# A third PSUM pair and an order by due times in a backward decode step of attention and gated MLP

## The chip, the cores and the metric

The kernel runs on one core of a Trainium2 chip. The metric is the device time of one execution in microseconds (us). Five engines work in parallel, each through its own queue in the order in which instructions were written: TensorE (PE, matmuls and weight loads), ScalarE (ACT), VectorE (DVE), GpSimd (POOL) and SyncE (SP, which here only issues DMAs). An instruction whose input or buffer isn't ready holds up everything behind it on its engine.

## The reference

For one decode token of two batches, output and all gradients of `x + attention(LN(x)) + MLP(LN(x))` are computed. The parts that carry the time:

```python
B, Sq, D, Hq, Hkv, Sk, Dh, F = 2, 1, 576, 32, 16, 4096, 128, 4608
scores = einsum("bhqd,bhkd->bhqk", q, k) * Dh**-0.5      # q = (xn @ wq), k, v: caches, each KV head for 2 query heads
o = einsum("bhqk,bhkd->bhqd", softmax(scores), v)        # attention = o @ wo
h = (xn @ w_gate) * (xn @ w_up)                          # MLP = h @ w_down
_out, _vjp = jax.vjp(f, x, k_cache, v_cache, wq, wo, w_gate, w_up, w_down)
return (_out, *_vjp(grad_out))
```

The caches are 2 x 16 x 4096 x 128 in bf16, 1 MB for each head and batch and cache. Their gradients are as large and are outer products: dV = p times dO, dK = dS times q. The gradients of the weights are outer products too.

## The kernel before, in words

**Steps.** The work on the caches is cut into 16 steps (`NS`): 8 groups of two KV heads (`G`), for each of the two batches. A step loads four tiles of 1 MB (`load_kv`, K and V of two heads, ring `kv` of 9 buffers), turns them on VectorE with 32-bit transposes (`turn`, ring `X` of 3), makes the scores of K (`score` with t=0, into PSUM tile `sk`) and the softmax (`softmax`), then the same product of V with dO (`dscore`, tile `sv`) and dS. `spread` brings p and dS into the forms `pp` and `dd` with small matmuls. `contract` then multiplies `pp` with V and `dd` with K, 128 matmuls, for the step's part of o and dq; only after it are the step's four `kv` buffers free for new loads. `outer` and `head_outer` make dV from `pp` and dK from `dd`: for each of 2 heads and 2 gradients four units (`unit`), 16 in a step. A unit takes a pair of PSUM banks (ring `o`, 2 pairs), fills it with two matmuls of 512 columns, and ScalarE or VectorE copies ("evicts") its 1024 columns to a store tile `st` (ring of 4). After four units the 1 MB tile is stored by SP. The right operand `BD` of the units is built by GpSimd, two for each step (L909).

**Weights.** Each group of heads also has a `group_front` (q and dO from the weights) and a `group_back` (gradients of wq and wo); nine `mlp` blocks of 512 columns of F do the MLP. Their outer products use the same `unit`s: `rows_unit` (576 columns), `cols_unit` (1024) and the tails (256).

**Small PSUM tiles.** The tiles `sk` and `sv` have a bank each; everything else that is small takes turns in ring `m` of two banks.

**What sets the order.** All functions are generators. `Order.run` simulates five engines with a fixed cost for each operation and writes the instructions in the order in which its simulated engines take them. Where several generators could go on at about the same time (`SLACK` 0.15), the lower priority number wins: scores and loads 0.0, stores 0.5, `contract` 1.0, `turn` 1.0, `mlp` 1.5, every outer unit 2.0. `EV` picks the engine of an eviction by the simulated time. Loads and stores of the caches share SP's queue (L810 and L477); loads of weights are on it as well; stores of weight gradients are on GpSimd's queue.

Of the kernel before, what the change touches and what calls it, by code (L numbers as in the profile page):

```python
# [13 lines left out]
P = 128  # L14
# [20 lines left out]
class Order:  # L35
# [3 lines left out]
    SLACK = 0.15  # L39

    def __init__(self):
        self.free = {e: 0.0 for e in ("PE", "ACT", "DVE", "POOL", "SP")}
        self.busy = dict(self.free)
        self.slots = {}
        self.dma = 0.0
        self.streams = []
        self.count = 0
        self.log = []
# [10 lines left out]
    def advance(self, s, value):  # L59
        while True:  # L60
# [13 lines left out]
            elif kind == "now":  # L74
                value = s.ready
# [31 lines left out]
    def run(self):  # L107
        while self.streams:
            cand = []
            for s in self.streams:  # L110
                t, e = self.start(s)
                if t is not None:
                    cand.append((t, s, e))
            assert cand, "no stream can go on: %s %s" % (
                [(x.gen.__name__, x.gen.gi_frame.f_lineno, x.ready, x.req) for x in self.streams], self.slots)
            t0 = min(c[0] for c in cand)
            t, s, e = min((c for c in cand if c[0] <= t0 + self.SLACK), key=lambda c: (c[1].prio, c[0]))
            r = s.req
            value = None
            if r[0] in ("op", "any"):  # L120
                cost = r[2] if r[0] == "op" else next(c for x, c, _ in r[1] if x == e)
                self.free[e] = t + cost
                self.busy[e] += cost
                s.ready = t + cost + self.HOP
                self.log.append((t, cost, e, s.prio))
# [9 lines left out]
            elif r[0] == "dma":  # L135
                self.free[e] = t + r[2]
                self.busy[e] += r[2]
# [3 lines left out]
                self.log.append((t, r[2], e, s.prio))  # L141
# [23 lines left out]
def EV(cols, bias=0.25):  # L165
    return ("any", [("ACT", 0.19 + cols * 0.00083, 0.0), ("DVE", 0.16 + cols * 0.00104, bias)])
# [21 lines left out]

def DMA(engine, cost, nbytes):
# [5 lines left out]
MLP0, MLPD = 5, 6.5  # L195
KVSTORE = "SP"


@with_exitstack
def kernel(  # L200
# [79 lines left out]
    osb_t = tiles("osb", 1, [P, P], FP32)  # L280
    od.ring("ch", 2)
    ch_t = []
    for i in range(2):
# [5 lines left out]
            pr=const.tile([P, P], BF16, name=f"pr{i}"), cs=const.tile([P, 1], FP32, name=f"cs{i}"),  # L289
            cr=const.tile([P, 1], FP32, name=f"cr{i}"), ds=const.tile([P, P], BF16, name=f"ds{i}")))  # L290
# [52 lines left out]
    for be in range(4):  # L343
        nc.vector.tensor_copy(sel[:, be], view(ident[:], 0, P, 64 * (be // 2) + be % 2, [[0, 4], [2, 32]]))
        nc.vector.tensor_copy(selA[:, be], view(ident[:], 0, P, 32 * be, [[0, 4], [1, 32]]))
    one1 = const.tile([1, 1], FP32, name="one1")
    nc.vector.memset(one1[:], 1.0)
    zer = const.tile([1, P], BF16, name="zer")
    nc.vector.memset(zer[:], 0.0)
# [12 lines left out]
    Wdy = const.tile([P, NB, 2, P], BF16, name="Wdy")  # L362
# [17 lines left out]
    def front():  # L380
# [37 lines left out]
        for src, dst in ((yb, dyr), (xnb, xnr)):  # L418
# [9 lines left out]
            if dst is dyr:  # L428
# [4 lines left out]
                for a in range(4):  # L433
                    nc.vector.tensor_copy(
                        view(Wdy[:], 32 * a, 32, 32 * a, [[P, 2 * NB], [1, 2]]), dyT[32 * a:32 * a + 32, :, 0:2])
# [28 lines left out]
    class Store:  # L464
        def __init__(self, n, out, after=None):
            self.n, self.out, self.after = n, out, after

        def done(self):
            self.n -= 1
            if self.n == 0:  # L470
                yield SPAWN(self.out(), (0.5,))
# [11 lines left out]
    def unit(mms, pe, cols, ev, store):  # L483
        i = yield ACQ("o")
        yield PE(pe)
# [19 lines left out]
    def rows_unit(a, lhs, st):  # L505
        def mms(o):
            for k in range(2):
                nc.tensor.matmul(o[:, k, 0:HD2], lhsT=lhs(a), rhs=dyr[32 * a:32 * a + 32, k * HD2:(k + 1) * HD2],  # L508
                                 start=True, stop=True)

        def ev(e, o):
            cp(e, st[:, a * D:(a + 1) * D].rearrange("p (k n) -> p k n", k=2), o[:, :, 0:HD2])
        return mms, 0.45, D, ev

    def rows_outer(lhs, dst, events=()):
# [3 lines left out]
        store = Store(FC, put("POOL", [(dst, src, 128 * FC * D * 2)], "st", i, events))  # L519
        for a in range(FC):  # L520
            yield SPAWN(unit(*rows_unit(a, lhs, st), store), (2.0,))

    def cols_outer(rhs, dst, events=()):
# [3 lines left out]
        store = Store(2, put("POOL", [(dst, src, 128 * 4 * FS * 2)], "st", i, events))  # L527
        for A in range(2):
            yield SPAWN(unit(*cols_unit(A, rhs, st, 0), store), (2.0,))

    def tail_outer(rhss, dsts, events=()):
# [4 lines left out]
        store = Store(2, put("POOL", parts, "tl", i, events))  # L536
# [12 lines left out]
        for A in range(2):  # L549
            yield SPAWN(unit(*mk(A), store), (2.0,))  # L550
# [6 lines left out]
    def mlp(i, Lgu, Ld, gs_slot, wd_slot):  # L557
# [26 lines left out]
        for k in range(NB):  # L584
            for e in range(2):
                nc.tensor.matmul(
                    dh, lhsT=Wdy[:, k, e, :], rhs=view(X[:], 0, P, 64 * k + e, [[D, FC], [2, 32]]),
# [10 lines left out]

        E = [Event() for _ in range(4)]
        yield SPAWN(rows_outer(lambda a: hb[32 * a:32 * a + 32, 0, :],  # L600
                               out_8[f0:f0 + FS, :].rearrange("(a p) n -> p a n", p=P), (E[0],)), (2.0,))
        for w, out in enumerate((out_6, out_7)):
            yield SPAWN(cols_outer(lambda a, w=w: hb[32 * a:32 * a + 32, 1 + w, :],
                                   out[0:512, f0:f0 + FS].rearrange("(c p) n -> p c n", p=P), (E[1 + w],)), (2.0,))
        yield SPAWN(tail_outer([lambda a, w=w: hb[32 * a:32 * a + 32, 1 + w, :] for w in range(2)],
                               [out[512:576, f0:f0 + FS] for out in (out_6, out_7)], (E[3],)), (2.0,))
# [18 lines left out]
        yield PE(1.6)  # L625
# [37 lines left out]
    def group_front(g):  # L663
# [7 lines left out]
        yield PE(1.6)  # L671
# [34 lines left out]
        for k in range(NB):  # L706
            for e in range(2):
                nc.tensor.matmul(
                    dp, lhsT=Wdy[:, k, e, :], rhs=view(X[:], 0, P, 64 * k + e, [[D, GH], [2, 32]]),
# [14 lines left out]
    def group_back(g):  # L724
# [9 lines left out]
        for t in range(2):  # L734
            for h in range(GH):
# [4 lines left out]
        E = [Event() for _ in range(3)]  # L740
        yield SPAWN(rows_outer(lambda a: R[32 * a:32 * a + 32, 0, :],
                               out_5[n0:n0 + FS, :].rearrange("(h p) n -> p h n", p=P), (E[0],)), (2.0,))
# [476 lines left out]
```

## Time and profile before

| | |
|---|---|
| median of 3 runs | 639.78 us (638.91 to 640.46) |
| profiled execution | 640.2 us, its span 638.4 us |
| mean granted TensorE clock | 0.584 of full |
| moved by DMA | 186.20 MB, mean 292 GB/s |
| evictions of 1024 columns | ScalarE 284, VectorE 24 |
| first and last `contract` matmul start | 42.7 and 578.3 us |

The span runs from the first to the last instruction. "Busy" is the time in which an engine had an instruction running; a group's line names the kernel's line, the engine, the operation, out<-in, and a count, then its busy time and the mean of one in ns, then the idle time of the engine just before and what ended it. In a timeline, the bracket gives the idle time before a row and its releaser; for SP a row can span the waits between the DMAs that it merges. "DMA share" is the mean busy share of the core's 16 DMA engines.

### The profile page before, as it was taken

What the parts mean: (1) busy time and instruction counts of PE and PEld (TensorE: products, weight loads), DVE (VectorE), ACT (ScalarE), POOL (GpSimd) and SP (SyncE); (2) the same over time, 40 slices, a digit from 0 to 9 for tenths busy, and PEclk for the clock granted to TensorE, in tenths of its full rate; (3) what the DMA queues carried; (4) which work ended last, traced back from release to release, by engine and by line L of the source; (5) the groups of instructions that cost most, each with busy time, mean ns of one, the idle gap of its engine ahead of it and who ended that gap; (6) DMA issues with size and microseconds to landing.
All of it is one profiled execution on the core that took longest, in us unless ns stands there. A gap on an engine that the chain in (4) does not pass through costs nothing. (4 is left out here: it accounts for less than half of the span.)

```text
span 638.4 us, 19297 instructions
## 1 busy us (share of the span) xinstructions
PE 452.2 (71%) x8489; PEld 270.5 (42%) x8489; DVE 355.1 (56%) x643; ACT 344.5 (54%) x470; POOL 204.8 (32%) x289
## 2 busy tenths in 40 slices
PE   1597676868767784778787775847687587978662
PEld 1475452635325452555354341424455454435210
DVE  8889631794227934688176552417395398344005
ACT  0124447564774664556544847656552176675890
POOL 4462033433314422343232323321154035332200
PEclk9976565765557565755555565655557555556555
DMA  8949989693998749986963969896938965493661
GB/s 314 377 165 360 381 322 411 234 382 144 364 390 353 295 179 397 373 334 191 393 282 137 402 269 397 315 377 254 333 135 328 378 229 208 181 343 150 243 268 78
DMA packets 47532, 186.20 MB, mean 292 GB/s; under 512 B 4396, under 2 KB 23992, under 8 KB 31064
## 3 DMA queue, kind: packets, MB, share of 16 engines
q1 hardware_dynamic: 40424, 159.61, 65.4%
q0 software_dynamic: 7024, 25.37, 10.4%
q8 instruction: 66, 1.08, 0.7%
q14 instruction: 18, 0.15, 0.1%
HBM read 92.48 MB, written 92.48 MB: 290 GB/s over the span
## 5 line engine op out<-in xcount | busy, mean ns | idle before, releaser
L309 ACT CAST st<-ps_o 128x1024 bf16<-128x1024 f32 (+1 forms) x345 | 310.6, 958 | 155.9 <-PE ps_o L953 74.8
L909 POOL TENSOR_TENSOR BD<-vr,mask 128x2048 bf16<-128x2048 bf16 x32 | 115.1, 3598 | 150.0 <-PE ps_o L953 102.5
L305 DVE STREAM_TRANSPOSE X<-kv 128x1024 f32<-128x1024 f32 x128 | 152.1, 1218 | 10.3 <-DMA kv<-in_A_k_cache_dram 6.0
L953 PE MATMUL ps_o<-BD,dd 32*128 32x512 bf16 x256 | 71.8, 592 | 31.1 <-ACT st L309 29.9
L953 PE MATMUL ps_o<-BD,pp 32*128 32x512 bf16 x256 | 68.5, 551 | 26.2 <-ACT st L309 25.5
L311 DVE CAST st<-ps_o 128x1024 bf16<-128x1024 f32 (+1 forms) x31 | 34.5, 1114 | 70.9 <-PE ps_o L508 29.3
L477 POOL DMA_DIRECT2D out_dram<-st x43 | 33.2, 771 | 94.1 <-ACT st L309 87.7
L921 PEld LDWEIGHTS <-W 128*32 128x32 bf16 x2048 | 50.4, 132 | 25.7 <-issue 22.7
L1092 PE MATMUL ps_m<-kv,dd 128*2 128x128 bf16 x1024 | 53.7, 286 | 5.0 <-issue 5.0
L1092 PE MATMUL ps_m<-kv,pp 128*2 128x128 bf16 x1024 | 53.6, 286 | 3.0 <-issue 3.0
L305 DVE STREAM_TRANSPOSE X<-ww 128x1152 f32<-128x1152 f32 x25 | 34.2, 1369 | 32.5 <-DMA ww<-in_B_w_down_dram 30.4
L1092 PEld LDWEIGHTS <-pp 128*2 128x2 bf16 x1024 | 45.0, 111 | 8.5 <-issue 7.0
L1092 PEld LDWEIGHTS <-dd 128*2 128x2 bf16 x1024 | 45.0, 111 | 5.9 <-issue 5.9
L953 PEld LDWEIGHTS <-dd 32*128 32x128 bf16 x256 | 15.0, 103 | 63.3 <-issue 57.5
L953 PEld LDWEIGHTS <-pp 32*128 32x128 bf16 x256 | 14.7, 99 | 58.8 <-issue 55.3
L888 POOL COPY W<-rep 32x16 bf16<-32x16 bf16 x128 | 24.5, 192 | 46.8 <-DVE rep L692 40.4
L921 PE MATMUL ps_sk<-X,W 128*32 128x128 bf16 x1024 | 31.7, 297 | 9.8 <-DVE X L305 9.2
L921 PE MATMUL ps_sv<-X,W 128*32 128x128 bf16 x1024 | 30.8, 296 | 4.0 <-DVE X L305 2.7
L448 POOL COPY wt<-wm 64x128 bf16<-64x128 bf16 (+1 forms) x34 | 8.9, 263 | 58.6 <-DVE wm L442 52.1
L477 POOL DMA_DIRECT2D out_dram<-tl x26 | 14.6, 563 | 33.0 <-ACT tl L309 33.0
L508 PE MATMUL ps_o<-dyr,R 32*128 32x288 bf16 x64 | 18.1, 394 | 9.0 <-ACT st L309 8.7
L309 ACT CAST vr<-ps_m 128x128 bf16<-128x128 f32 x19 | 5.1, 268 | 35.2 <-PE ps_m L901 35.2
(178 smaller groups left out, 593.3 us busy)
## 6 DMA issues: line engine op xcount, KB each, us to landing
out_dram<-st SPq DMA_DIRECT2D x64, 1024.0 KB, 6.1
kv<-in_A_k_cache_dram SPq DMA_DIRECT2D x32, 1024.0 KB, 11.3
kv<-in_A_v_cache_dram SPq DMA_DIRECT2D x32, 1024.0 KB, 9.5
out_dram<-st POOLq DMA_DIRECT2D x26, 512.0 KB, 7.7
out_dram<-st POOLq DMA_DIRECT2D x17, 576.0 KB, 8.1
ww<-in_B_w_down_dram SPq DMA_DIRECT2D x9, 576.0 KB, 8.3
ww<-in_A_wo_dram SPq DMA_DIRECT2D x8, 576.0 KB, 7.9
gu<-in_B_w_gate_dram SPq DMA_DIRECT2D x9, 512.0 KB, 10.0
```

Source lines behind the costliest of these rows:

```text
L305: nc.vector.transpose(out, in_)
L309: nc.scalar.copy(out, in_)
L311: nc.vector.tensor_copy(out=out, in_=in_)
L448: nc.gpsimd.tensor_copy(view(Wt[:], 64 * h, 64, 0, [[dims[-1][1], n], [1, dims[-1][1]]]), view(Wm[:], 64 * h, 64, off, dims))
L477: (nc.gpsimd if engine == "POOL" else nc.sync).dma_start(dst, src)
L508: nc.tensor.matmul(o[:, k, 0:HD2], lhsT=lhs(a), rhs=dyr[32 * a:32 * a + 32, k * HD2:(k + 1) * HD2], start=True, stop=True)
L888: nc.gpsimd.tensor_copy(view(W_t[t][w][:], 32 * a, 32, 6 + 8 * a, [[G * WW, 4], [WW, G], [1, 2]]), view(rep_t[grp[g]["qs"]][:], 32 * a, 32 ...
L909: nc.gpsimd.tensor_tensor(BD_t[i][:], view(vr_t[v][:], 0, P, 0, [[0, 16], [1, Dh]]), view(mask16[:], 0, P, 0, [[1, 16], [0, Dh]]), ALU.mult)
L921: nc.tensor.matmul(sc[32 * cq:32 * cq + 32, :], lhsT=view(W[:], 0, P, (be * G + l) * WW + 6 - 4 * c2 - 2 * l, [[1, 32]]), rhs=view(X[:], 0 ...
L953: nc.tensor.matmul(o[:, k, :], lhsT=pr2[32 * c4:32 * c4 + 32, :], rhs=BD[32 * c4:32 * c4 + 32, 8 * l + 4 * h2:8 * l + 4 * h2 + 4, :], star ...
L1092: nc.tensor.matmul(ct[32 * j:32 * j + 2, 0:P], lhsT=rT[:, 4 * c + 2 * l:4 * c + 2 * l + 2], rhs=kv_t[slot][:, Dh * c:Dh * (c + 1)], start= ...
```

## The change

**Third pair.** The tiles `sk` and `sv` are gone, and ring `o` has three pairs. The scores now lie in ring `m`. So that a score tile is read from PSUM once, the maximum is taken by an operation that also copies the tile to `ex` in SBUF, and the exponential works there in place. In `dscore` the tile is read once into `ed` (`ex` times dP), and dS comes from two VectorE operations on SBUF tiles.

**Quadrants.** A unit of dK or dV uses row quadrants 0 and 1 or 2 and 3 of TensorE. Units now alternate between the two halves, and the planner counts the second of such a pair at 0.12. `rows_unit` takes two quadrants where it took one twice.

**Fewer small products.** `contract` uses 32 columns of the weights for each head and no longer a zero matmul ahead. The transpose after it is in bf16, its two copies are one. `Wdy` is stored overlapped.

**Order.** Each stage of each step has a due time, `STEP * s + PR[name]`, as its priority; the two queues of weight loads are apart; `SLACK` is a number for each engine, and the planner takes the earliest start first. `turn` and the evictions are placed by it too.

```diff
-            t0 = min(c[0] for c in cand)
-            t, s, e = min((c for c in cand if c[0] <= t0 + self.SLACK), key=lambda c: (c[1].prio, c[0]))
+            t, _, s, e = min(cand, key=lambda c: c[:2])
+            if e is not None:
+                t, _, s, e = min((c for c in cand if c[3] == e and c[0] <= t + SLACK[e]), key=lambda c: (c[1], c[0]))
...
+                quad = r[3] if len(r) > 3 else None
+                if quad is not None and self.quad == (1 - quad, t):
+                    cost = 0.12
...
-MLP0, MLPD = 5, 6.5
+MLP0, MLPD = 4, 6.15
...
+STEP = 28.0
+PR = {"turn0": 78.6, "turn1": 48.6, "att": -16.9, "dsc": 2.7, "con": 21.9, "out1": 12.2, "out0": 66.9, "front": -23.9,
...
+def pr(name, s):
+    return STEP * s + PR[name]
...
-    o_t = banks("o", 2, [P, 2, 512])
+    o_t = banks("o", 3, [P, 2, 512])
     m_t = banks("m", 2, [P, 512])
-    sk_t = banks("sk", 1, [P, P])
-    sv_t = banks("sv", 1, [P, P])
...
-    def rows_unit(a, lhs, st):
+    def rows_unit(j, lhs, st):
+        A, k = divmod(j, 2)
+
         def mms(o):
-            for k in range(2):
-                nc.tensor.matmul(o[:, k, 0:HD2], lhsT=lhs(a), rhs=dyr[32 * a:32 * a + 32, k * HD2:(k + 1) * HD2],
+            for aa in range(2):
+                a = 2 * A + aa
+                nc.tensor.matmul(o[:, aa, 0:HD2], lhsT=lhs(a), rhs=dyr[32 * a:32 * a + 32, k * HD2:(k + 1) * HD2],
                                  start=True, stop=True)
...
-        for A in range(2):
-            for h2 in range(2):
-                yield SPAWN(one(A, h2), (2.0,))
+        for h2 in range(2):
+            for A in range(2):
+                yield SPAWN(one(A, h2), pr(f"out{t}", s))
...
-        nc.vector.reduce_max(c["mx"][:], sc[:], axis=AX.X)
+        nc.vector.tensor_tensor_reduce(
+            out=c["ex"][:], in0=sc, in1=view(zero1[:], 0, P, 0, [[0, P]]), scale=1.0, scalar=-3.0e38,
+            op0=ALU.add, op1=ALU.max, accum_out=c["mx"][:],
+        )
+        yield REL("m", k)
...
-        nc.scalar.activation(c["ex"][:], sc[:], AF.Exp, bias=c["negb"][:], scale=SCALE, accum_out=c["z"][:])
-        yield REL("sk", k)
+        nc.scalar.activation(c["ex"][:], c["ex"][:], AF.Exp, bias=c["negb"][:], scale=SCALE, accum_out=c["z"][:])
...
-        nc.vector.scalar_tensor_tensor(out=c["ds"][:], in0=dp[:], scalar=c["cr"][:], in1=c["pr"][:],
-                                       op0=ALU.subtract, op1=ALU.mult)
-        yield REL("sv", k)
+        nc.vector.scalar_tensor_tensor(out=c["ed"][:], in0=c["ex"][:], scalar=c["cr"][:], in1=c["ed"][:],
+                                       op0=ALU.mult, op1=ALU.subtract)
+        yield DVE(0.22)
+        nc.vector.tensor_scalar(c["ds"][:], c["ed"][:], c["rz"][:], -1.0, op0=ALU.mult, op1=ALU.mult)
...
-            if part == 0:
-                nc.tensor.matmul(ct[:, 0:P], lhsT=zer[:], rhs=zer[:], start=True, stop=True, skip_group_check=True)
...
-                    nc.tensor.matmul(ct[32 * j:32 * j + 2, 0:P], lhsT=rT[:, 4 * c + 2 * l:4 * c + 2 * l + 2],
-                                     rhs=kv_t[slot][:, Dh * c:Dh * (c + 1)], start=False,
-                                     stop=(c == NCH - 1), skip_group_check=True)
+                    nc.tensor.matmul(ct[32 * j:32 * j + 32, 0:P], lhsT=view(rT, 0, P, 4 * c + 2 * l, [[1, 32]]),
+                                     rhs=kv_t[slot][:, Dh * c:Dh * (c + 1)], start=(c == 0), stop=(c == NCH - 1))
```

What this moves is seen best on three queues. On TensorE, before, `contract` of step 8 (L1092) stands there whole, and its end is followed by other work and then the first unit (L953):

```order
L1092 LDWEIGHTS dd_120
L1092 MATMUL ps_m_148<-kv_61,dd_120 2x128
L901 LDWEIGHTS qr_111
L901 MATMUL ps_m_147<-ident,qr_111 128x128
L953 LDWEIGHTS pp_119
L953 MATMUL ps_o_145<-BD_88,pp_119 128x512
```

With the change, in the same step, units of the step's own dV (L978) stand between the quarters of `contract` (L1119):

```order
L1119 LDWEIGHTS dd_120
L1119 MATMUL ps_m_150<-kv_61,dd_120 32x128
L978 LDWEIGHTS pp_118
L978 MATMUL ps_o_147<-BD_87,pp_118 128x512
...
L1119 LDWEIGHTS pp_118
L1119 MATMUL ps_m_150<-kv_62,pp_118 32x128
```

The units of a step, which before stood up to a step and a half later, now stand inside and right behind that step's `contract`; behind the last `contract` of all stand 16 matmuls of such units, where 62 stood.

On SP, before, around the loads of the same part of the program (`kv` with L810 are loads of the caches, L477 are stores):

```order
L477 DMA out_dram<-st_83 128x4096
L477 DMA out_dram<-st_80 128x4096
L810 DMA kv_64<-in_A_k_cache_dram 128x4096
L810 DMA kv_65<-in_A_v_cache_dram 128x4096
L810 DMA kv_66<-in_A_v_cache_dram 128x4096
L810 DMA kv_68<-in_A_k_cache_dram 128x4096
L477 DMA out_dram<-st_81 128x4096
L477 DMA out_dram<-st_82 128x4096
```

With the change (L836 loads, L497 stores, L859 and L876 loads of weights):

```order
L836 DMA kv_64<-in_A_k_cache_dram 128x4096
L497 DMA out_dram<-st_81 128x4096
L836 DMA kv_65<-in_A_v_cache_dram 128x4096
L836 DMA kv_66<-in_A_v_cache_dram 128x4096
L836 DMA kv_69<-in_A_k_cache_dram 128x4096
L497 DMA out_dram<-st_80 128x4096
L859 DMA ww_76<-in_A_wo_dram 128x4x576
L876 DMA ww_78<-in_B_w_down_dram 128x2304
L497 DMA out_dram<-st_83 128x4096
```

Loads and stores alternate instead of standing in blocks, and from step 4 to step 12 the same sequence recurs every two steps.

On VectorE, before, the end of `dscore` (L1046 to L1057) is one piece, with the dP tile `ps_sv` read twice:

```order
L1046 ISA ds_144,cs_142<-ex_138,ps_sv_150 128x128
L1046 ISA cs_142 128x1
L1054 TENSOR_TENSOR cr_143<-ps_m_147,rz_140 128x1
L1057 SCALAR_TENSOR_TENSOR ds_144<-ps_sv_150,cr_143,pr_141 128x128
L1108 CAST oT_107<-ps_m_147 128x4
L1110 TENSOR_SCALAR oT_107<-ps_m_147 128x4
```

With the change it has one operation more (L1087), its last two read SBUF alone, and transposes (L321) stand between them:

```order
L1081 TENSOR_TENSOR cr_133<-ps_m_151,rz_129 128x1
L321 STREAM_TRANSPOSE X_70<-kv_64 128x1024
L806 TENSOR_TENSOR accx<-accx,ps_m_151 128x160
L1084 SCALAR_TENSOR_TENSOR ed_132<-ex_127,cr_133,ed_132 128x128
L321 STREAM_TRANSPOSE X_72<-kv_65 128x1024
L1087 TENSOR_SCALAR ds_134<-ed_132,rz_129 128x128
```

Over the whole program VectorE now has 81 of the 308 evictions of 1024 columns and ScalarE 227; before, 24 and 284. Of those of 576 columns VectorE has 13 (7 before), of the tails 4 (10 before).

More of the change, by code (lines that the diff above doesn't have):

```diff
@@ L194 @@
 NKV, NX, NGU, NWW, NST, NBD = 9, 3, 1, 5, 4, 3
-MLP0, MLPD = 5, 6.5
+MLP0, MLPD = 4, 6.15
 KVSTORE = "SP"
+WQ0, WO0 = -7, 0
+BIAS = 0.24
+SLACK = {"PE": 0.18, "ACT": 0.12, "DVE": 0, "POOL": 0.35, "SP": 0}
+STEP = 28.0
+PR = {"turn0": 78.6, "turn1": 48.6, "att": -16.9, "dsc": 2.7, "con": 21.9, "out1": 12.2, "out0": 66.9, "front": -23.9,
+      "back": 57.7, "W0": -10.7, "W1": -20.2, "BD1": -3.2, "BD0": 3.7, "mlp": -8.5, "wout": -14.3, "store": -74.7,
+      "load": -16.5, "wload": -142.9, "mload": -9.9}
+def pr(name, s):
+    return STEP * s + PR[name]
 @with_exitstack
```

198 lines of the change are left out of this document (103 added, 95 removed).

## The prediction

> **What bounds the kernel now.** I read the page first: no engine is near its span.
>
> ```profile
> span 638.4 us, 19297 instructions
> PE 452.2 (71%) x8489; PEld 270.5 (42%) x8489; DVE 355.1 (56%) x643; ACT 344.5 (54%) x470; POOL 204.8 (32%) x289
> ...
> DMA  8949989693998749986963969896938965493661
> ...
> q1 hardware_dynamic: 40424, 159.61, 65.4%
> q0 software_dynamic: 7024, 25.37, 10.4%
> q8 instruction: 66, 1.08, 0.7%
> q14 instruction: 18, 0.15, 0.1%
> ```
>
> The resource used most is DMA: its queues sum to 76.6% of 638.4, that is 489 us busy and 149 idle. The row of tenths alternates between 9 and 3 to 6. So I read the windows: three near the ends of the run, one full stretch, then the gaps between 120 and 160 us.
>
> ```profile
> 0.00:4.00 4.00, 0.00 (x0) 0.00 (x0) 2.16 (x9) 1.28 (x1) 3.42 (x16) 1.00 0.37 114
> 40.00:48.00 8.00, 7.72 (x250) 5.59 (x236) 7.98 (x8) 3.43 (x6) 5.85 (x14) 0.65 0.02 4
> 600.00:638.00 38.00, 18.82 (x97) 5.08 (x92) 9.25 (x21) 22.25 (x26) 3.79 (x5) 0.50 0.47 184
> ...
> 240.00:280.00 40.00, 26.57 (x502) 16.95 (x500) 23.00 (x41) 19.91 (x27) 12.18 (x24) 0.59 1.03 384
> ...
> 120.00:122.00 2.00, 2.00 (x113) 1.82 (x105) 0.29 (x1) 0.00 (x0) 0.27 (x1) 0.83 0.03 8
> 122.00:124.00 2.00, 2.00 (x115) 1.54 (x99) 0.53 (x2) 0.37 (x1) 0.00 (x0) 1.00 0.04 8
> 142.00:144.00 2.00, 2.00 (x64) 1.55 (x65) 1.22 (x5) 0.88 (x1) 0.00 (x0) 0.50 0.40 168
> 144.00:146.00 2.00, 2.00 (x81) 1.37 (x66) 1.96 (x2) 0.58 (x3) 0.00 (x0) 0.50 0.04 12
> 146.00:148.00 2.00, 1.92 (x25) 0.73 (x22) 1.25 (x5) 1.85 (x3) 0.00 (x0) 0.50 0.00 0
> 156.00:158.00 2.00, 1.35 (x52) 1.16 (x41) 0.00 (x0) 0.00 (x0) 0.85 (x2) 0.50 0.32 74
> 158.00:160.00 2.00, 1.42 (x38) 0.91 (x37) 0.35 (x2) 0.58 (x1) 0.00 (x0) 0.94 0.03 8
> ```
>
> The last two columns are DMA share and GB/s. Idle at the ends: 4 x 0.63 = 2.5 us at the start, 8 x 0.98 = 7.8 before the first stores, 38 x 0.53 = 20.1 at the end. The other 119 us lie between, in gaps like the three shown: 3.9 us at 120, 5.1 at 142, 3.3 at 156. During the first and the last ScalarE is idle and TensorE isn't. SP's timeline says why.
>
> ```profile
> 101.99 14.83 SPq L477 DMA_DIRECT2D out_dram<-st  x4
> 123.00 0.34 SPq L810 DMA_DIRECT2D kv<-in_A_k_cache_dram  x1
> ```
>
> After four stores, the last of which goes out at 116.8, nothing is issued until a load at 123.00: loads wait until `contract` frees their buffers, and while `contract` runs as a block TensorE fills no unit, so no store comes due. The gap at 142 has another origin, VectorE:
>
> ```profile
> 137.92 3.58 DVE L592 TENSOR_TENSOR hb<-gs 128x128 bf16<-128x128 f32 x1
> ...
> 137.76 3.60 POOL L909 TENSOR_TENSOR BD<-vr,mask 128x2048 bf16<-128x2048 bf16 x1 [7.97 <-PE ps_o L953]
> ...
> 141.89 0.59 PE L1052 MATMUL ps_m<-cs,G 128*128 128x1 f32 x2 [3.37 <-DVE hb L594]
> ```
>
> An operation whose median is 0.27 us took 3.58 because GpSimd's `BD` build began 0.16 us earlier; TensorE stood 3.37 us behind it, and 5.1 us of DMA were lost. I call this a lock stall. How often it happens, from minimum/median/maximum and from the means:
>
> ```profile
> L592 DVE TENSOR_TENSOR hb<-gs x9: 247/269/3579, 48.0 to 573.9; 128x128 bf16<-128x128 f32 x9
> L1020 DVE TENSOR_SCALAR pr<-ex,rz x16: 246/288/3515, 34.8 to 536.9; 128x128 bf16<-128x128 f32 x16
> L1004 DVE COPY mr<-m x16: 173/215/2714, 24.7 to 533.1; 1x128 f32<-1x128 f32 x16
> L1057 DVE SCALAR_TENSOR_TENSOR ds<-ps_sv,cr,pr x16: 308/351/351, 37.2 to 544.9; 128x128 bf16<-128x128 f32 x16
> ...
> L1020 DVE TENSOR_SCALAR pr<-ex,rz 128x128 bf16<-128x128 f32 x16 | 17.1, 1071 | 1.2
> L1004 DVE COPY mr<-m 1x128 f32<-1x128 f32 x16 | 9.1, 566 | 0.4
> L592 DVE TENSOR_TENSOR hb<-gs 128x128 bf16<-128x128 f32 x9 | 5.9, 650 | 0.0
> ```
>
> Above their medians: 17.1 - 16 x 0.288 = 12.5, 9.1 - 16 x 0.215 = 5.7, 5.9 - 9 x 0.269 = 3.5, together 21.7 us. L1057, which reads a PSUM tile, never exceeded 0.351.
>
> The page SBUF — State Buffer of the Trainium skill (Who interferes with whom) states that a VectorE instruction with two SBUF inputs, or a copy or tensor_scalar in a two-port mode, shares an exclusive port lock with GpSimd. The rows of `hb` agree.
>
> **The change, part by part.** *Units inside `contract`* (the order of TensorE): this removes the gaps beside it. At the mean of the two seen, 3.6 us, over 16 steps, 57 of the 119 us go. Bounds: none, if the units there lack a store tile, to all 57.
>
> *Third pair and alternate quadrants.* In a run of units ScalarE sets the pace:
>
> ```profile
> L309 ACT CAST st<-ps_o 128x1024 bf16<-128x1024 f32 x284 | 273.2, 1026 | 105.6 <-PE ps_o L953 74.8 <-DMA out_dram<-st 18.8 <-PE ps_o L497 5.2
> L311 DVE CAST st<-ps_o 128x1024 bf16<-128x1024 f32 x24 | 29.2, 1218 | 39.3 <-DMA out_dram<-st 18.6 <-PE ps_o L953 9.5 <-ACT st L309 5.3
> ...
> 101.10 0.61 PE L953 MATMUL ps_o<-BD,pp 32*128 32x512 bf16 x2 [0.31 <-ACT st L309]
> 102.02 0.61 PE L953 MATMUL ps_o<-BD,pp 32*128 32x512 bf16 x2 [0.31 <-ACT st L309]
> ```
>
> Units start 0.92 us apart, TensorE works 0.61 of it. A faster pair of matmuls alone therefore buys nothing; I cost it at zero, with ScalarE's copy as the cover. What helps is that VectorE takes 81 copies rather than 24. ScalarE falls by 57 x 1.026 = 58 us to about 286; VectorE gains 57 x 1.218 = 69. The few 576-column and tail copies that change places I leave out.
>
> *VectorE's other work.* L1087 is new and of the kind of `pr`: 16 x 1.071 = 17.1 us (bounds by its minimum and maximum: 3.9 and 56). L1084 now has two SBUF inputs, like `hb`: 16 x (0.650 - 0.351) = 4.8 (bounds: -1.7 by `hb`'s minimum, +52 by its maximum). The 16 second copies of `oT` are too small for a term. VectorE's sum is 355 + 69 + 17 + 5 = 446 us. The lock stalls rise by 12.5, as `pr`, and 16 x (0.650 - 0.269) = 6.1, as `hb`: from 21.7 to 40.3 us. Queued behind each are evictions, the small chain and the transposes; TensorE waits for all three.
>
> By that page's rule alone, a 3.6 us build twice a step would meet an operation with chance 32 x 3.6 / 638 = 0.18 and hold it 1.8 us on average, 32 x 0.18 x 1.8 = 10 us for the 32 operations, an estimate below the 18.6 that the rows give.
>
> *Smaller products.* `contract` has the same 2048 matmuls with 32 instead of 2 columns. The nearest rows are its own and the scores', which have 32:
>
> ```profile
> 0.00:638.00 638.00, 54.09 (x2048) 45.47 (x2048) 0.58 0.77 292
> ...
> 0.00:638.00 638.00, 62.42 (x2048) 50.40 (x2048) 0.58 0.77 292
> ```
>
> So 0 to +8 us on TensorE, against 16 zero matmuls gone. The bf16 transpose also saves there. TensorE, busy 452 before, has no more to do than it had; nothing on the path.
>
> *The end.* Units with 62 matmuls stood behind the last `contract`, 31 copies; 16 now, 8 copies. The 23 copies, at 0.92 us, took 21 us there, but their stores must still be made earlier, so this moves DMA work and doesn't remove it. What stays is the last store and the closing chain, 638.4 - 623.3 = 15 us:
>
> ```profile
> 622.23 1.09 ACT st L309
> ...
> 623.34 0.33 SPq L477
> ```
>
> I keep the 20.1 us of idle DMA at the end, and 7.8 and 2.5 at the start.
>
> *Order by due times.* Of the 119 us, 57 lie beside `contract` and 21.7 x 5.1 / 3.37 = 33 follow lock stalls; the other 29 I put down to blocks of loads and stores, which the new SP order breaks up (bounds: 0 to 29 gone). Two queues are passed: weight loads now stand between stores on SP, and a store that isn't ready holds them; the ring of five weight tiles is their cover, and if that is short, `mlp` waits.
>
> **Sum.** What stays of the 119 is the lock stalls, 40.3 us at between 1 and 1.5 us of DMA each: 40 to 61, I take 50. 489 + 2.5 + 7.8 + 20.1 + 50 = 569.4 of span, +1.8 for what lies around it (640.2 - 638.4) = 571.2. The profiled run was 0.4 above the median of the three, so 571.
>
> The page DMA: Bandwidth & Descriptors of the Trainium skill (Specifications) gives a limit of about 358 GB/s for HBM per core. The row 240 to 280 shows 384, so the measurement decides; by that limit the 186.2 MB alone would take 520 us, which would lift the DMA-bound rival below to about 552 and leave the forecast.
>
> **The rivals.** *DMA-bound:* the stalls fall where a transfer covers them. 10 us stay: 489 + 30.4 + 10 + 1.8 = 531. For it: DMA shares of 1.0 over long stretches; against: VectorE at 446 of 530 us in strict order. Chance 0.13.
>
> *Half smoothing:* only the gaps beside `contract` go, and the new stalls come on top: 119 - 57 + 18.6 x 1.5 = 90 stay, giving 611. For it: the planner's costs know neither the lock nor late transfers. Chance 0.18.
>
> *The change doesn't do what it says:* score tiles in the two banks of `m` block the small products, and TensorE loses in waits what the third pair gives; the gaps stay as they are, about 639. Against: the scores hold a bank for some 2 us, 32 times, in an order planned for it. Chance 0.04.
>
> *VectorE becomes the bound, slower:* it was idle 638 - 355 = 283 us, mostly waiting for inputs. Evictions now stand in its queue behind transposes that wait for loads; TensorE waits for the pair, `contract` ends later, loads start later, and the next transposes wait again. With 446 us of work the time is above 640 if more than 640 - 1.8 - 446 = 192 of its 283 us of waits remain. At three quarters, 212: 660. Against: these waits are for work that now comes evenly. Chance 0.08.
>
> **How the numbers follow.** The forecast's own case, 0.57, spans 545 to 600 by 25 to 79 us of idle kept. The range takes in the DMA-bound and most of the half-smoothed case: 526 to 622. About 0.2% is what a measurement here can tell from no change. Faster: 0.57 + 0.13 + 0.18 = 0.88; same 0.04; slower 0.08.
>
> **What would show it.** The steps now begin, by the first and last start of `contract`, (578.3 - 42.7) / 15 = 35.7 us apart:
>
> ```profile
> L1092 PE MATMUL ps_m<-kv,dd x1024: 217/311/314, 42.7 to 578.3; 128*2 128x128 bf16 x171
> ```
>
> In the profile after: DMA share about 0.86; no window of 2 us at share 0.04 beside `contract`; first `contract` near 43 us, then steps of about 32 us; VectorE busy about 446 and ScalarE 286; the new L1087 with a maximum near 3.5 us, and TensorE waits behind it. I am wrong if the gaps beside `contract` persist, or if VectorE's waits stay above 192 us.

## The result, and the profile after

The changed kernel takes 510.68 us (median of 4 runs, 509.37 to 511.46), the kernel before beside it 639.35 (635.59 to 640.46): ratio 0.7994, 95% interval 0.7956 to 0.8032. The profiled execution took 509.37 us. The page, first the lines that answer to those of before:

```profile
span 507.5 us, 19218 instructions
PE 372.3 (73%) x8457; PEld 246.1 (48%) x8457; DVE 443.5 (87%) x711; ACT 288.9 (57%) x420; POOL 203.4 (40%) x289
...
DMA  7993999999999999999999999999999999999793
...
q1 hardware_dynamic: 40424, 159.61, 81.6%
q0 software_dynamic: 7024, 25.37, 12.8%
q8 instruction: 66, 1.08, 0.8%
q14 instruction: 18, 0.15, 0.1%
```

The queues sum to 95.3% of 507.5: 484 us busy (489 before), 24 idle (149 before). So nearly the whole gain, some 125 of 131 us of span, is idle time of the DMA engines. The windows say where the rest of it lies (last two columns: DMA share, GB/s):

```profile
0.00:4.00 4.00, 0.00 (x0) 0.00 (x0) 2.32 (x8) 1.28 (x1) 3.37 (x17) 1.00 0.35 120
40.00:48.00 8.00, 5.26 (x144) 3.77 (x147) 8.00 (x10) 4.25 (x6) 3.60 (x1) 0.67 0.33 133
120.00:160.00 40.00, 31.12 (x735) 20.19 (x732) 35.34 (x51) 22.40 (x33) 14.26 (x23) 0.63 1.03 410
240.00:280.00 40.00, 31.23 (x742) 20.16 (x739) 36.93 (x54) 22.46 (x33) 14.67 (x19) 0.59 1.02 398
480.00:507.00 27.00, 15.81 (x303) 8.75 (x302) 21.15 (x36) 13.28 (x17) 2.96 (x6) 0.63 0.69 270
```

2.6 us are idle at the start, 8 x 0.67 = 5.4 before the first stores and 27 x 0.31 = 8.4 at the end; that leaves 24 - 16.4, some 7 us, for everything between, where 119 lay. The stretch from 120 to 160, where three gaps were shown before, now has a share of 1.03. The steps follow from the first and last start of `contract`, and the copies from their groups:

```profile
L1119 PE MATMUL ps_m<-kv,pp x1024: 218/313/315, 45.9 to 485.5; 128*32 128x128 bf16 x171
```

```profile
L325 ACT CAST st<-ps_o 128x1024 bf16<-128x1024 f32 x227 | 219.8, 1019 | 91.6 <-PE ps_o L978 39.6 <-DMA out_dram<-st 34.7 <-PE ps_o L517 10.2
L327 DVE CAST st<-ps_o 128x1024 bf16<-128x1024 f32 x81 | 97.7, 1207 | 24.0 <-DMA out_dram<-st 11.9 <-ACT st L325 5.3 <-issue 3.5
```

(485.5 - 45.9) / 15 = 29.3 us for a step, and 22 us behind the last one (60 before). The lock stalls, with minimum/median/maximum and then the groups' sums:

```profile
L1084 DVE SCALAR_TENSOR_TENSOR ed<-ex,cr,ed x16: 301/2318/3696, 40.6 to 475.0; 128x128 f32<-128x128 f32 x16
L1048 DVE TENSOR_SCALAR pr<-ex,rz x16: 244/1966/2326, 31.0 to 469.4; 128x128 bf16<-128x128 f32 x16
L1087 DVE TENSOR_SCALAR ds<-ed,rz x16: 235/242/2504, 42.1 to 475.6; 128x128 bf16<-128x128 f32 x16
```

```profile
L1084 DVE SCALAR_TENSOR_TENSOR ed<-ex,cr,ed 128x128 f32<-128x128 f32 x16 | 28.2, 1760 | 0.0
L1048 DVE TENSOR_SCALAR pr<-ex,rz 128x128 bf16<-128x128 f32 x16 | 25.7, 1604 | 0.0
L1087 DVE TENSOR_SCALAR ds<-ed,rz 128x128 bf16<-128x128 f32 x16 | 12.9, 808 | 0.0
```

Above 16 times their minima these three alone have 23.4 + 21.8 + 9.1 = 54 us, against 40.3 forecast for all. For `pr` and for L1084 the stall is now the median. The trace shows what they wait for: 25 of the 48 executions take over 1.5 us, and every one of these ends 0.07 to 0.15 us after a `BD` build on GpSimd does. The stalls grew, and yet the DMA engines hardly idle.

### The profile page after: what moved, and what is told of

The parts are those of the page before. It is cut to its first block, busy times and chain, and to the rows that moved or that the text cites. A ratio compares the mean times of both kernels' runs of the same rounds, so it can differ in the third digit from the quotient of the medians.

```text
span 507.5 us, 19218 instructions
## 1 busy us (share of the span) xinstructions
PE 372.3 (73%) x8457; PEld 246.1 (48%) x8457; DVE 443.5 (87%) x711; ACT 288.9 (57%) x420; POOL 203.4 (40%) x289
## 2 busy tenths in 40 slices
DMA packets 47532, 186.20 MB, mean 367 GB/s; under 512 B 4396, under 2 KB 23992, under 8 KB 31064
## 4 chain that ended last, share of the span: by engine, by line
DMA 43%; PE 28%; DVE 12%; ACT 9%; issue 6%; SPq 2%; ACTq 0%; DVEq 0%
DMA out_dram<-st 36%; ACT st L325 8%; PE ps_m L1119 7%; PE ps_o L978 7%; DVE st L327 4%; PE ps_m L945 3%; DVE X L321 3%; DMA gu<-in_B_w_up_dram 3%; DMA kv<-in_A_v_cache_dram 2%; DMA kv<-in_A_k_cache_dram 2%; PE ps_m L609 2%; PE ps_o L531 2%; SPq L854 1%; DVE ds L1087 1%; DVE ed L1084 1%
## 5 line engine op out<-in xcount | busy, mean ns | idle before, releaser
L325 ACT CAST st<-ps_o 128x1024 bf16<-128x1024 f32 (+1 forms) x282 | 252.2, 946 | 96.7 <-PE ps_o L978 39.6
L321 DVE STREAM_TRANSPOSE X<-kv 128x1024 f32<-128x1024 f32 x128 | 155.6, 1225 | 0.9 <-DMA kv<-in_A_k_cache_dram 0.5
L327 DVE CAST st<-ps_o 128x1024 bf16<-128x1024 f32 (+1 forms) x94 | 107.2, 1142 | 25.7 <-DMA out_dram<-st 11.9
L945 PE MATMUL ps_m<-X,W 128*32 128x128 bf16 x2048 | 62.7, 296 | 9.4 <-issue 5.0
L978 PE MATMUL ps_o<-BD,pp 32*128 32x512 bf16 x256 | 53.7, 555 | 17.9 <-ACT st L325 17.3
L497 POOL DMA_DIRECT2D out_dram<-st x43 | 33.5, 779 | 73.0 <-ACT tl L325 32.9
L1119 PE MATMUL ps_m<-kv,dd 128*32 128x128 bf16 x1024 | 58.7, 293 | 3.6 <-issue 3.6
L1119 PE MATMUL ps_m<-kv,pp 128*32 128x128 bf16 x1024 | 58.7, 292 | 0.0
L945 PEld LDWEIGHTS <-W 128*32 128x32 bf16 x2048 | 50.1, 132 | 16.8 <-issue 15.6
L1119 PEld LDWEIGHTS <-pp 128*32 128x32 bf16 x1024 | 46.5, 133 | 23.3 <-issue 21.9
L978 PE MATMUL ps_o<-BD,dd 32*128 32x512 bf16 x256 | 47.2, 518 | 11.7 <-ACT st L325 6.5
L1119 PEld LDWEIGHTS <-dd 128*32 128x32 bf16 x1024 | 46.5, 133 | 2.1 <-issue 2.1
L321 DVE STREAM_TRANSPOSE X<-ww 128x1152 f32<-128x1152 f32 x25 | 34.1, 1363 | 6.6 <-PE ps_m L945 5.0
L978 PEld LDWEIGHTS <-pp 32*128 32x128 bf16 x256 | 13.7, 106 | 30.7 <-issue 28.7
L1084 DVE SCALAR_TENSOR_TENSOR ed<-ex,cr,ed 128x128 f32<-128x128 f32 x16 | 28.2, 1760 | 0.0
L1048 DVE TENSOR_SCALAR pr<-ex,rz 128x128 bf16<-128x128 f32 x16 | 25.7, 1604 | 0.0
L321 DVE STREAM_TRANSPOSE X<-gu 128x1024 f32<-128x1024 f32 x18 | 21.9, 1221 | 0.5 <-PE ps_m L945 0.5
L978 PEld LDWEIGHTS <-dd 32*128 32x128 bf16 x256 | 10.3, 97 | 20.8 <-issue 17.2
```

The lines of the kernel that those rows point to most:

```text
L321: nc.vector.transpose(out, in_)
L325: nc.scalar.copy(out, in_)
L327: nc.vector.tensor_copy(out=out, in_=in_)
L497: (nc.gpsimd if engine == "POOL" else nc.sync).dma_start(dst, src)
L945: nc.tensor.matmul(sc[32 * cq:32 * cq + 32, :], lhsT=view(W[:], 0, P, (be * G + l) * WW + 6 - 4 * c2 - 2 * l, [[1, 32]]), rhs=view(X[:], 0 ...
L978: nc.tensor.matmul(o[:, k, :], lhsT=pr2[32 * c4:32 * c4 + 32, :], rhs=BD[32 * c4:32 * c4 + 32, 8 * l + 4 * h2:8 * l + 4 * h2 + 4, :], star ...
```

## The experiments

Three theories stood at first. Theory 1: the order keeps the DMA fed. Theory 2: the third pair and VectorE's copies decouple TensorE from ScalarE. Theory 3: less work on TensorE. Since most edits make the planner order all engines anew, later runs separate what acts on the chip from what acts through the plan. In each run the kernel before was timed on the same chip, at medians of 637.3 to 640.5 us. "Idle" is the DMA engines' in the profiled run, worked out as above.

| run | us | ratio, 95% interval | DMA busy, idle |
|---|---|---|---|
| all but the order | 585.57 | 0.916, 0.9077 to 0.9243 | 488, 99 |
| order alone | 596.52 | 0.9334, 0.9261 to 0.9408 | 490, 103 |
| two pairs | 570.96 | 0.8933, 0.8868 to 0.8998 | 488, 81 |
| old units | 547.34 | 0.8555, 0.8481 to 0.8628 | 484, 65 |
| third pair alone | 590.14 | 0.9234, 0.9189 to 0.9278 | 487, 103 |
| alternation alone | 624.42 | 0.9761, 0.971 to 0.9813 | 489, 135 |
| halves exchanged | 513.27 | 0.8025, 0.7981 to 0.8069 | 485, 30 |
| same quadrants | 512.55 | 0.8029, 0.7982 to 0.8077 | 484, 27 |
| half of dK stored | 497.53 | 0.7793, 0.7755 to 0.7831 | 450, 44 |
| dP read twice | 526.5 | 0.8256, 0.8214 to 0.8298 | 483, 40 |
| L1087 twice | 510.61 | 0.801, 0.7967 to 0.8052 | 484, 26 |
| copies on ScalarE | 545.45 | 0.8548, 0.8507 to 0.859 | 486, 55 |
| plan unaware of short units | 535.85 | 0.8384, 0.833 to 0.8439 | 480, 55 |
| third pair unplanned | 563.28 | 0.8809, 0.8728 to 0.889 | 487, 77 |
| bias 0.20 | 541.61 | 0.8479, 0.8417 to 0.8542 | 485, 53 |
| bias 0.28 | 524.06 | 0.8215, 0.8159 to 0.8271 | 482, 40 |
| before, bias 0.21 | 639.23 | 1.0003, 0.9954 to 1.0052 | 488, 151 |
| before, bias 0.29 | 637.03 | 0.9992, 0.9947 to 1.0038 | 488, 150 |

Wherever all bytes are moved, busy stays at 480 to 490 us; the runs differ in idle time.

**All but the order, and the order alone.** The first has the old priorities, `SLACK` 0.15 and one weight queue; the second has the due times and, of the rest, only small edits that are named below.

```diff
-    return STEP * s + PR[name]
+    return PR[name]
```

```diff
+            t, _, s, e = min(cand, key=lambda c: c[:2])
+            if e is not None:
+                t, _, s, e = min((c for c in cand if c[3] == e and c[0] <= t + SLACK[e]), key=lambda c: (c[1], c[0]))
```

> Keeps all of the change but the order: constant priorities, one slack of 0.15 and one queue of weight loads as before. Theory 1 (the order keeps DMA fed): DMA gaps come back, 600 to 640 us, DMA share below 0.82. Theory 2 (third pair and VectorE's share of the evictions decouple TensorE): 520 to 560. Theory 3 (less TensorE work): 520 to 560 too.

> The order by due times alone: two pairs, own banks for the scores and their old reading, old units and old contract. Theory 1: 510 to 550 us, DMA share above 0.88. Theory 2: 590 to 640. Theory 3: 570 to 640.

Measured 585.57, which lies between all the ranges, and 596.52, which lies outside Theory 1's. The first gives 54 of the 129 us and the second 43; both together give 32 more than their sum. No single theory holds; Theory 1 in its strict form fell with the second run.

"Alone" needs a reservation, here and for the two runs with one part alone below. Beside the part that is named, all three kernels have the change's bf16 transpose with one copy, its overlapped `Wdy` and the planner's new costs (3.6 us for a `BD` build in place of 4.5, for one). No run has these without a part, so their share of the 43, and of the gains below, is not known. Their pages suggest that it is not nothing: TensorE was busy 452 us before and is busy 422 to 424 us in the three.

**Two pairs, old units.** Each leaves one part of the change out, with a new plan.

```diff
-    o_t = banks("o", 3, [P, 2, 512])
+    o_t = banks("o", 2, [P, 2, 512])
```

```diff
-        for h2 in range(2):
-            for A in range(2):
+        for A in range(2):
+            for h2 in range(2):
```

> The change with two PSUM pairs for the units in place of three, two banks unused. Theory 1: 505 to 526 us. Theory 2: above 555.

> The change with the units in the old order of halves, the row units in one quadrant. Theories 1 and 2: 507 to 518 us, since evictions and DMA cover TensorE. Theory 3: 530 or more.

They lose 60 us, as Theory 2 has it, and 37, as Theory 3 has it, against the changed kernel, so both parts, which the prediction costed at zero, seemed to matter.

**Third pair alone, alternation alone.** The kernel before, with its old rules of order, one part and the small edits named above.

```diff
-    o_t = banks("o", 2, [P, 2, 512])
+    o_t = banks("o", 3, [P, 2, 512])
...
-    sk_t = banks("sk", 1, [P, P])
-    sv_t = banks("sv", 1, [P, P])
```

```diff
-        for A in range(2):
-            for h2 in range(2):
+        for h2 in range(2):
+            for A in range(2):
```

> The kernel before with the third pair of PSUM banks and what frees them (score tiles in the small ring, read once); old order, old units, old small products. Theory P (the wait of TensorE for a free pair holds up all that is queued behind it, so the pair acts without the order too): about 640 minus 25 to 40, 600 to 615 us, and VectorE takes evictions. Theory R (the third pair pays only in an order that has work for it): 630 to 642 us.

> The kernel before with the new units alone: two pairs, the old score banks, the old order and small products, but the units of a head and the row units alternate between the two quadrant pairs. Theory P (TensorE's row is what everything waits in): 610 to 628 us. Theory R, the one of the prediction (with two pairs ScalarE's copy is the longer half of each unit and covers the product, so a faster product alone gives nothing): 634 to 642 us, with units shorter all the same.

The first run is 49 us faster than the kernel before, more than either theory allowed. TensorE's longest waits for the copies, before:

```profile
PE ps_o L953 <- ACT st L309: 55.4, 101, 6.3
PE ps_o L508 <- ACT st L309: 11.2, 20, 2.8
```

and with the third pair alone, after the line of the engines:

```profile
PE 422.5 (72%) x8473; PEld 260.7 (44%) x8473; DVE 403.3 (68%) x683; ACT 318.5 (54%) x449; POOL 203.0 (34%) x289
```

```profile
PE ps_o L973 <- ACT st L322: 26.7, 56, 3.0
PE ps_o L527 <- ACT st L322: 14.9, 13, 10.1
```

67 us of waits fall to 42. ScalarE has 257 of the large copies where it had 284; this run can't tell what of the 49 us is the pair, what those copies and what the small edits. The run with alternation is 15 us faster, which is in Theory P's range and not in that of the prediction; but what of the 15 is the alternation is as open. TensorE's time for the units of dK and dV is 139 us before, 133 with alternation alone, 122 with the third pair alone and 101 in the changed kernel, so alternation alone accounts for little of that fall.

**Halves exchanged, same quadrants.** The changed kernel's plan, instruction for instruction; only which quadrants a unit uses is altered. The first let units of two heads still alternate; the second takes, of what the head has left, a part in the quadrants used last:

```diff
-            yield from unit(*mk(A, h2), store, A)
+            yield from unit(*mk(h2, A), store, A)
```

```diff
+                A, h2 = min(left, key=lambda u: (u[0] != last[0], u))
```

> The changed kernel with its planned order untouched, instruction for instruction, but in the units of a head the tile's two halves and the two quadrant pairs change places, so that every other unit of a head multiplies in the quadrants of the unit before it; the result of a head is the same. Theory P (the quadrants act on the chip: TensorE's time for the units falls and the rest of TensorE's row moves up): units take 15 to 25 us more of TensorE, and the time rises to 525 to 545 us. Theory R (what the kernel with the old units lost, 37 us, was the planner's other order, and TensorE's units lie beside the DMA): 510 to 516 us, with units just as much longer.

> Like the earlier exchange of halves, in which the units of two heads still alternated by turns: the changed kernel's planned order, instruction for instruction, but each unit of a head takes, of what its head has left, a part in the quadrants of the unit before it, whichever head that was. Units take 15 to 30 us more of TensorE than the changed kernel's 100.9 us, else nothing is told. Theory P (TensorE's faster units set the time): 520 to 540 us. Theory R (with three pairs the units' own length is covered; what the old units lost came with the planner's other order): 508 to 515 us.

TensorE's time for all units, changed kernel and second run (the third number):

```profile
0.00:507.00 507.00, 100.88 (x512) 23.96 (x512) 0.66 0.95 367
```

```profile
0.00:510.00 510.00, 108.26 (x512) 24.54 (x512) 0.66 0.95 365
```

The units take 5 us more in the first run (105.50) and 7 in the second, not 15 to 30, and the time rises by 3 and 2 us, within the intervals. How many units then do follow one in their own quadrants was not counted. In this order the choice between these sequences of quadrants is worth next to nothing on the chip.

**Plan unaware of short units; third pair unplanned.** The first keeps the instructions and lets the planner book 0.45 us for every unit; the second keeps the plan for two pairs, and the units take three in turn.

```diff
-            yield from unit(*mk(A, h2), store, A)
+            yield from unit(*mk(A, h2), store)
...
-        mms(o_t[i])
+        o = o3_t[used[0] % 3]
+        used[0] += 1
+        mms(o)
```

> The changed kernel with its instructions, but the planner isn't told that a unit in the other quadrants is short: it books 0.45 us for every unit of a head and orders all engines by that. Theory P (what the alternation gives comes on the chip): 508 to 516 us. Theory R (it comes from the plan, which packs the units more closely when it books them short): toward the 547 us of the kernel with the old units, 530 to 550 us.

> The plan of the kernel with two pairs, instruction for instruction, but the units use three pairs in turn, so that TensorE may run one unit further ahead of the copies than the plan knows. Theory P (the wait for a free pair on the chip is what two pairs cost): most of the 60 us come back, 510 to 530 us, and TensorE's waits for the copies nearly vanish. Theory R (the plan made for two pairs has the copies and the transfers late whatever TensorE may do): 555 to 572 us.

The same instructions in the other plan lose 25 us. The third pair given to the two-pair plan returns 8 of its 60 us; both times lie in Theory R's ranges. TensorE's waits with two pairs and with the unplanned third:

```profile
PE ps_o L978 <- ACT st L325: 32.3, 68, 4.1
PE ps_o L531 <- ACT st L325: 16.7, 15, 4.9
```

```profile
PE ps_o L982 <- ACT st L327: 22.0, 44, 4.0
PE ps_o L535 <- ACT st L327: 12.7, 10, 3.9
```

So in these plans both parts act mainly through the order that the planner makes of them.

**One number of the planner.** That raised the question how far plans of the same work lie apart.

```diff
-BIAS = 0.24
+BIAS = 0.20
...
-def EV(cols, bias=0.25):
+def EV(cols, bias=0.21):
```

> The changed kernel with one number of the planner altered, the bias against VectorE's copies 0.20 in place of 0.24: the plan is another, the work the same, some copies more on VectorE. This is the measure of what a new plan alone does. Theory N (single plans scatter widely): 10 us or more from the changed kernel's 511, to either side, 495 to 530 us. Theory S (plans of the same work lie close): 507 to 515 us.

> The same with the bias at 0.28, some copies more on ScalarE. Theory N: 10 us or more away from 511 us, 495 to 530 us, slower most likely, since 0.24 was chosen. Theory S: 507 to 515 us.

> The kernel before with one number of its planner altered: the bias against VectorE's copies 0.21 in place of 0.25. If plans of the kernel before scatter as widely as those of the changed kernel (511, 524 and 542 us at biases of 0.24, 0.28 and 0.20), its 639 us is itself one draw: 610 to 655 us, 8 us or more away. If its order, which has no due times, hardly answers to such a number: 633 to 645 us.

> The same with the bias at 0.29: 610 to 655 us, 8 us or more away, if plans scatter here too; 633 to 645 us if not.

In the changed kernel 0.20 costs 31 us and 0.28 costs 13, as Theory N has it, though 0.20 comes out slower than its range. The number does more than shift copies: VectorE has 81 large ones at 0.24, 63 at 0.28 and, against what was expected, only 75 at 0.20. In the kernel before nothing can be measured; but there VectorE has 26 and 21 of them for 24, so its plan may simply have moved too little to show a scatter. In the 0.20 plan two stretches are thin:

```profile
200.00:240.00 40.00, 29.66 (x659) 19.91 (x659) 29.23 (x51) 21.73 (x36) 15.04 (x12) 0.59 0.82 316
280.00:320.00 40.00, 30.95 (x585) 18.79 (x585) 33.53 (x50) 26.63 (x36) 20.01 (x22) 0.54 0.81 301
```

the same stretches of the changed kernel are not:

```profile
200.00:240.00 40.00, 30.64 (x671) 20.46 (x672) 34.23 (x53) 22.73 (x35) 16.02 (x22) 0.54 0.97 376
280.00:320.00 40.00, 31.06 (x692) 20.43 (x690) 33.56 (x54) 25.85 (x38) 18.30 (x27) 0.67 1.00 378
```

What SP waited for between 200 and 240 in the 0.20 plan:

```profile
SPq L497 <- ACT st L325: 18.3, 3, 12.2
SPq L836 <- PE ps_m L1119: 9.1, 1, 9.1
```

and in the changed kernel:

```profile
SPq L497 <- DVE st L327: 10.9, 1, 10.9
SPq L850 <- PE ps_m L652: 6.5, 1, 6.5
```

In the 0.20 plan a store waited 12.2 us at the head of SP's queue for a copy by ScalarE, and the load right behind it 9.1 us for `contract`. SP issued that one store, at 222 us, between 209 and 231, and from 228 to 232 the DMA share is 0.00. In the changed kernel SP waits almost as long for a store, but the load follows 2.7 us behind it, at 226, and from 204 to 236 us no 4 us have a share below 0.83. In the second thin stretch four stores hold the queue from 279 to 300 us, and the loads stand behind them.

**What bounds the changed kernel.** Four edits: half of each dK tile isn't stored (16.8 MB of output left out); the dP tile read twice as before; one locked operation doubled; all copies from the pairs on ScalarE.

```diff
+                                   (oviews[t][b, G * g + l][:, 0:2048], st[:, 0:2048], 1 << 20)]
...
+        nc.vector.scalar_tensor_tensor(out=c["ds"][:], in0=dp, scalar=c["cr"][:], in1=c["pr"][:],
...
+        for _ in range(2):
+            nc.vector.tensor_scalar(c["ds"][:], c["ed"][:], c["rz"][:], -1.0, op0=ALU.mult, op1=ALU.mult)
...
+BIAS = 50.0
```

> The changed kernel, but of each tile of the K cache's gradient only the first half is stored: 16.8 of 186.2 MB are left out, and that half of the output is not written. Theory D (the changed kernel is bound by its transfers, 484 us of them busy at 186.2 MB): 16.8 MB at the mean 367 to 385 GB/s are 44 to 46 us, so 464 to 472 us. Theory V (VectorE with 443 us of work and its waits ends close behind): 485 to 505 us. Theory O (the order of the engines sets the time): 505 to 511 us.

> The changed kernel, but the second score tile stays in its bank and is read there twice, as before: the two operations on VectorE that wait longest behind GpSimd's builds (28.2 and 12.9 us) give way to one that took 5.6 us before, and the bank of the small ring is held about 2 us longer. The planner orders it anew. Theory V (the changed kernel waits for VectorE's row, 443 of 507 us busy): VectorE falls to about 408 us and the time by 10 to 30 us, 480 to 500 us. Theory D (the transfers bind, 484 us busy): 502 to 512 us. Theory M (the small ring is what holds things up): slower, 515 to 530 us.

> The changed kernel's order, but one of the operations on VectorE that GpSimd's builds hold up (L1087, 12.9 us in all, 235 ns when free) is issued twice in each step; the second writes the same values. VectorE gets 4 to 13 us more. Theory V: all of it shows, 514 to 524 us. Theory D: 509 to 513 us.

> The changed kernel with a bias in the planner so high that every copy out of the pairs falls to ScalarE: the third pair stays, but VectorE takes none of its copies. VectorE falls by about 98 us to 346, ScalarE rises to about 365. The prediction's theory (the copies that VectorE takes are what the third pair brings): the time goes back to what two pairs gave, 560 to 590 us. Theory P (the third pair itself lets TensorE run ahead, whoever copies): 505 to 530 us.

With half of dK stored the page reads:

```profile
PE 375.3 (76%) x8457; PEld 249.4 (50%) x8457; DVE 445.1 (90%) x711; ACT 288.6 (58%) x420; POOL 203.5 (41%) x289
...
q1 hardware_dynamic: 40424, 142.83, 76.9%
q0 software_dynamic: 7024, 25.37, 13.3%
```

33 us of transfers go, fewer than the 44 to 46 that were expected; 20 come back as idle time, and 13 are gained. The time, 497.53, is in Theory V's range and far from Theory D's. So the transfers alone don't set the time of the changed kernel: once they are shorter by 13 us, something else binds, VectorE (90% busy here) or the order, and this run doesn't tell which. The doubled operation:

```profile
PE 377.7 (74%) x8457; PEld 249.1 (49%) x8457; DVE 449.4 (88%) x727; ACT 288.7 (57%) x420; POOL 204.1 (40%) x289
```

```profile
L1088 DVE TENSOR_SCALAR ds<-ed,rz 128x128 bf16<-128x128 f32 x32 | 16.0, 501 | 0.6
```

The operation takes 16.0 us where it took 12.9, VectorE in all 5.9 more, and the time doesn't move: Theory D's range, not Theory V's. The test is weak, though: with the same work in the same order VectorE was busy 440 to 445 us in other runs, and the intervals leave room for some 4 us. Reading dP twice takes VectorE from 443 to 409 us and costs 16 us, which fits Theory M by its number; but it is also a new plan, and a new plan alone costs 13 and 31. With all copies on ScalarE the time is 545.45, between the two theories' ranges and, again, near the plan with bias 0.20. No run that computes everything was measurably faster than the changed kernel.

## Why the prediction was wrong

The forecast was 571 us, between 526 and 622; 511 were measured, below all of that. Neither of the two signs of being wrong that it gave appeared: it erred to the other side.

**Right.** That the transfers are the resource used most, the size of their busy time (489 forecast, 484), that the gaps beside `contract` go, ScalarE's sum (286; 288.9), and that 32 columns in `contract` cost 0 to 8 us (59.3 for 54.1).

**Right in part by luck: VectorE's sum** (446; 443.5). Its three locked operations take 66.8 us where the terms gave 44.6. The sum comes out all the same because the terms are rows added up, while busy time counts records that overlap once: VectorE's rows add up to 487 us for 443.5 busy, and before to 381 for 355.1.

**Wrong: what stays of the 119.** The step "the lock stalls, 40.3 us at between 1 and 1.5 us of DMA each: 40 to 61, I take 50" failed. The factor came from one gap of before, at 142 us, where TensorE stood behind the stall and no transfer was left to run. In the changed kernel the stalls of three operations sum to 54 us, and some 7 us are idle between the ends for all causes. Nor does less stall go with less idle time: with the bias at 0.28, at 0.20 and with the plan unaware of short units these operations take 46.4, 40.5 and 37.7 us in place of 66.8, and the DMA engines idle 40, 53 and 55 us in place of 24. So the prediction took the price of a stall from the order that the change removes. Of the 62 us by which its span was too long, this is 43 (50 - 7); the ends are 14, the busy time 5. It is also what lies between the steps that were forecast, 32 us, and those measured, 29.3: (32 - 29.3) x 15 = 41. That transfers issued earlier cover the stalls is the reading of this; the doubled operation, its only test, is a weak one.

**Wrong: the ends.** "I keep the 20.1 us of idle DMA at the end, and 7.8 and 2.5 at the start": measured 8.4, 5.4 and 2.6, together 14 us less; 22 us follow the last `contract` instead of 60. The DMA work that was said to be only moved into the middle found room there.

**Right in part: third pair and alternation at zero.** In the changed kernel's order the quadrants are worth 2 or 3 us on the chip, near the nothing that was said. The third pair was probably under-rated: 49 us in the old order with the small edits, 34 more than alternation gave with the same edits. With it VectorE has 51 large copies in place of 24, so the copies that the prediction counted apart come in part with the pair.

**Mis-sized: the locked operations.** L1084 was costed like `hb` at 16 x 0.650 = 10.4 us and takes 28.2; `pr` rose from 17.1 to 25.7; L1087 was put at 17.1 and takes 12.9. The page SBUF — State Buffer of the Trainium skill (Who interferes with whom) says that such operations and GpSimd exclude each other; L1084 with 301 ns at the least and 3696 at the most, just above one 3.6 us build, agrees. The estimate of 10 us by chance meetings was too small because in this order they are no chance: `pr` is held up by a build in 12 of the 16 steps, and L1084 or L1087 in 13.

**The rivals.** DMA-bound (531), with a chance of 0.13, comes nearest, with its stalls that fall where a transfer covers them. It kept too much, 10 us between and 30.4 at the ends, where 7 and 16.4 were measured. (With 520 us of transfers it would have given 562, not 552: there its own 10 us were forgotten.) Half smoothing and VectorE as a slower bound didn't occur; VectorE's idle time is 64 us.

**What no step held.** The plan itself. With bias 0.20 or 0.28 the change gives 541.61 or 524.06. The losses of 37, 35, 25 and 16 us in single edits are no larger than, or near, what a new plan does without any edit; only the 60 of two pairs and the 75 of the old order stand well above. How the 129 us divide among the parts therefore stays open beyond this: the order gives 43 and the rest 54 each alone, the third pair 49 in the old order, the 43 and the 49 with the small edits in them, and 13 to 31 of the whole may belong to this one plan, whose number had been chosen. Why the plan at 0.24 has no thin stretch was read from two windows, not shown by an experiment.

## What to carry to other kernels

Price a stall by what is queued ahead of it in the order that will be, not in the one that is. Where a planner orders the instructions, time two or three neighbours of its numbers before giving any part of a change the credit; here they differ by 13 and 31 us with the same work. A kernel with "one part alone" needs a kernel beside it that has everything else of it. To see what a part does on the chip, keep the plan and change the part; to see what it does through the plan, keep the part and lie to the planner.

## What was not expected of the hardware

The page DMA: Bandwidth & Descriptors of the Trainium skill (Specifications) has about 358 GB/s as the limit of HBM for a core. The changed kernel moves 367 GB/s on the mean of its whole span and 410 from 120 to 160 us, so that figure is no ceiling here.

Leaving out half of each dK store took 9% of the bytes (169.43 for 186.20 MB) and 7% of the busy time (484 to 450 us).

Units that take, where they can, the quadrants of the unit before cost TensorE only 7 us over 256 units, 108.26 for 100.88.

Whether an operation of VectorE stalls is a matter of some 0.2 us: in the changed kernel L1084 took 0.34 us the three times that it began 0.16 to 0.24 us before a `BD` build, and 2.0 to 3.7 us the nine times that it began during one.
